# A windowed attention and two MLPs: first values in three loads of whole rows held twice, keys of the second group earlier, table load between loads

## The chip, the cores and the metric

The kernel runs on one core of a Trainium2 chip. A core has five engines with instruction streams of their own: TensorE (PE; its weight loads are listed as PEld), VectorE (DVE), ScalarE (ACT), GpSimd (POOL) and SyncE (SP), which here only issues loads and stores. The metric is the time of one execution on the device in microseconds, and the number compared is the median of the timed runs. One further execution was recorded by the hardware profiler.

## The reference

```python
scores = scale * np.matmul(q, k.transpose(0, 1, 3, 2))      # B,H,S,D = 4, 8, 576, 64
mask = (rel >= 0) & (rel < 128)                             # rel = query - key position
scores = np.where(mask, scores + bias[None], -1000000000.0) # bias = -slope[h] * |rel|
...
attn = attn / (np.sum(attn, axis=-1, keepdims=True) + 1e-09)
attn_out = np.matmul(attn, v)
x = attn_out.transpose(0, 2, 1, 3).reshape(2304, 512)
h = x @ moe_w_in;  x = np.maximum(0.01 * h, h) @ moe_w_out          # 512 -> 2048 -> 512
h = x @ moe2_w_in; y = (h * (1 / (1 + np.exp(-1.702 * h)))) @ moe2_w_out
```

Each query sees the 128 keys up to its own position. The weights of the two MLPs are given as 64-bit words.

## The kernel before, in words

**Attention.** The batches are taken in order; the 8 heads of a batch form two groups of four. The work of a group is cut into four parts of the 576 queries, so there are 32 steps (`steps`). The first eight steps take group 0 and group 1 of batch 0 in turns: steps 0, 2, 4, 6 are group 0, steps 1, 3, 5, 7 group 1. Step 0 and step 1 need the first 256 keys and queries of their group, steps 2 and 3 the rest.

A step is a pipeline over three turns of the loop at L533: in turn s, TensorE computes the scores of step s (`att_scores`, L253), the products with the values of step s-3 (`att_av`, L337) and the transposes of the softmax weights of step s-2 (`att_trans`, L302). VectorE adds the bias and takes the row maximum (`att_ttr`, L271), ScalarE takes the exponential (`att_exp`, L283), VectorE and GpSimd divide by the sum. The two transposed tiles of a step are copied from PSUM to the tile `pt` (`att_evac`): the first always by ScalarE (L310), the second by ScalarE in turns below 9 and by VectorE from turn 9 on (L312).

**Weights.** The raw blocks of the MLP weights (`raw`, 512 KB each, L115) are converted by nine operations spread over ScalarE, VectorE and GpSimd (`conv_w`, L136 to L148). In the attention's turns a turn starts a conversion where its number is in `convs`, and one group of MLP products of the first two chunks goes behind the attention's work of the turn. After the attention the MLP products fill TensorE (`steady`).

**Order of the work.** From L532 on the instructions stand on each engine in the order in which the code is written. What stands ahead of it (first loads, constants, warm-up products) is ordered by the framework. Each engine takes its instructions strictly in order, the queues of SyncE and ScalarE for loads as well. The framework gives the loads of both queues, in turn, eight completion counters; a load on a counter waits until the load that had this counter before has landed.

**The first loads.** `load_first` (L210) issues, on SyncE and ScalarE, queries and keys of group 0 (first part), of group 1 (first part), the rest of group 0, a raw block, the values of group 0, the rest of group 1, a raw block and the values of group 1. `q` comes in pieces of 64 numbers, 64 partitions to a load (L179). `k` comes with 128 partitions to a load (L185). The values of a group come in eight loads (L206): for each pair of heads, each head and each half of the 128 rows of a block, the rows of 64 numbers go to the 64 partitions at which the product with the weights wants them. A pair's two heads want the same keys at different halves of the partitions, so that the four products of a block can run on different quarters of TensorE's array. `values[b, g]` is the tile, and L339 picks `vv[r, a, kb]` from it.

The tile `ys` is the output of the MLPs; as long as it holds none, its columns serve as buffers: `late` holds queries, keys and values of the first group of batch 1, `kbuf` the keys, others are scratch of the conversions. The pool tag `v` has two buffers.

```python
    vv = (late[:, 2].rearrange("p a (n d) -> p a n d", d=64) if n == 2 else
          sb([128, 2, NKB, 64], F32, "v", 2))
```

Of the kernel before, what the change touches and what calls it, by code (L numbers as in the profile page):

```python
# [7 lines left out]
F32 = mybir.dt.float32  # L8
# [3 lines left out]
AF = mybir.ActivationFunctionType  # L12
ALU = mybir.AluOpType

B, H, S, D = 4, 8, 576, 64
# [5 lines left out]
CB = 2  # L21
# [3 lines left out]
NKB = S // 64  # L25
# [6 lines left out]
def attention_mlp_kernel(  # L32
        ctx: ExitStack, tc: tile.TileContext, qin, kin, v, w1i, w1o, w2i, w2o, out):
    nc = tc.nc
# [5 lines left out]
    def sb(shape, dt, tag, bufs):  # L40
        return pool.tile(shape, dt, tag=tag, name=tag, bufs=bufs)

    def ps(tag):
        return psum.tile([128, 512], F32, tag=tag, name=tag, bufs=2)
# [9 lines left out]
    def tick():  # L54
        step[0] += 1
        for fn in later.pop(step[0], []):
            fn()
# [12 lines left out]
    ys = const.tile([128, NT * 4], F32, name="y")  # L70
# [41 lines left out]
    def load_w(n, p):  # L112
        layer, f = divmod(n, NF)
        raw = sb([128, 1024], U32, "raw", 2)
        nc.sync.dma_start(out=raw, in_=wsrc[layer][p][f].bitcast(U32))  # L115
        wraw[n, p] = raw

    def alloc_w(n):
        wt[n] = wt[n - 2 * CB] if n >= 2 * CB else sb(
            [128, 4, 512], F32R, "wA" if n < CB else "wB", CB)  # L120
# [43 lines left out]
    qkv, values = {}, {}  # L164


    late = ys[:, 2560:2560 + 6 * S].rearrange("p (n a s) -> p n a s", n=3, a=2)

    def new_qk(n):
        qkv[divmod(n, 2)] = ((late[:, 0], late[:, 1]) if n == 2 else  # L170
                             (sb([128, 2, S], F32, "q", 2), kbuf[:, n % 2]))


    def load_q(e, n, a, lo, hi):
        b, g = divmod(n, 2)
        for h in range(2):
            d = slice(64 * h, 64 * h + 64)
            src = qin[b, 2 * g + a, d].rearrange("p (m h q) -> p m h q", h=2, q=64)
            e.dma_start(  # L179
                out=qkv[b, g][0][d, a, 64 * lo:64 * hi].rearrange("p (m q) -> p m q", q=64),  # L180
                in_=src[:, lo:hi, h])

    def load_k(n, lo, hi):
        b, g = divmod(n, 2)
        nc.sync.dma_start(  # L185
            out=qkv[b, g][1][:, :, 64 * lo:64 * hi],
            in_=kin[b, 2 * g:2 * g + 2, :, 64 * lo:64 * hi].rearrange("a p s -> p a s"))

    def load_qk(n):
        new_qk(n)  # L190
        for a in range(2):
            load_q(nc.sync, n, a, 0, NKB)
        load_k(n, 0, NKB)

    def load_v(n):
        b, g = divmod(n, 2)
        vv = (late[:, 2].rearrange("p a (n d) -> p a n d", d=64) if n == 2 else
              sb([128, 2, NKB, 64], F32, "v", 2))
        values[b, g] = vv

        for a in range(2):
            for h in range(2):
                for r in range(2):
                    src = v[b, 2 * g + a, 64 * r:64 * r + 64, 0:NQB - r, 64 * h:64 * h + 64]
                    k0 = 64 * (h ^ a)
                    nc.sync.dma_start(out=vv[k0:k0 + 64, a, r::2], in_=src)  # L206

    def load_first():  # L210
        for n in range(2):
            new_qk(n)
        load_q(nc.sync, 0, 0, 0, 4)
        load_q(nc.scalar, 0, 1, 0, 4)
        load_k(0, 0, 4)
        load_q(nc.scalar, 1, 0, 0, 4)
        load_q(nc.sync, 1, 1, 0, 4)
        load_k(1, 0, 4)
        for a in range(2):
            load_q(nc.scalar, 0, a, 4, NKB)  # L220
        load_k(0, 4, NKB)
        load_w(*wload.pop())
        load_v(0)
        for a in range(2):
            load_q(nc.sync, 1, a, 4, NKB)
        load_k(1, 4, NKB)
        load_w(*wload.pop())
        load_v(1)

    sp, sm, pp, pt, ot = {}, {}, {}, {}, {}  # L230
# [76 lines left out]
    def att_evac(s, n, e):  # L307
        t = sb([128, 384], F32, "pt", 3)
        if e is nc.scalar:
            nc.scalar.activation(t, pp.pop((s, n))[:, 0:384], AF.Copy)  # L310
        else:
            nc.vector.tensor_copy(t, pp.pop((s, n))[:, 0:384])  # L312
        pt[s, n] = t
# [4 lines left out]
    def att_av(s):  # L318
        b, g, i = steps[s]
        vv = values[b, g]  # L320
        ot[s] = [ps("O") for _ in range(2)]
        if i:
            todo = [(2 * i - 2 + c, 128 * c - (64 if c > 0 else 0), 128 * c + (64 if c < 3 else 0),
                     0 if c > 0 else 64, x == 0, x == 3) for x, c in enumerate((1, 2, 0, 3))]
        else:
            todo = [(m - w + 1 + c, 128 * (c0 + c), 0, 64 * x, c == 0, c == w - 1)
                    for x, (m, (_, w, c0)) in enumerate(zip((0, 1, 8), ENDS)) for c in range(w)]
        for kb, c0, c1, o0, start, stop in todo:
            for a in range(2):
                for h in range(2):  # L330
                    r = slice(64 * (h ^ a), 64 * (h ^ a) + 64)
                    if i:
                        rhs = pt[s, a][r, c0:c1]
                    else:
                        n, c = divmod(c0, 384)
                        rhs = pt[s, n][r, c + 64 * a:c + 64 * a + 64]
                    nc.tensor.matmul(  # L337
                        out=ot[s][a][64 * h:64 * h + 64, o0:o0 + rhs.shape[-1]],
                        lhsT=vv[r, a, kb], rhs=rhs, start=start, stop=stop,  # L339
                        skip_group_check=True,  # L340
                    )

# [174 lines left out]
            tick()  # L517


    wz = sb([128, 384], F32, "pt", 3)  # L520
    nc.gpsimd.memset(wz, 0.0)
    wp = ps("mm")
    for _ in range(6):
        nc.tensor.matmul(
            out=wp[:, 0:256], lhsT=wz[:, 0:128], rhs=wz[:, 128:384], start=True, stop=True)
    load_first()
    emit_consts()
    for n in range(2 * CB):
        alloc_w(n)
    convs = (0, 2, 4, 5, 7, 8, 10, 11)  # L530
    nconv, credit = 0, 0.0
    with tc.manual_schedule():  # L532
        for s in range(NS + 3):  # L533
            tick()
            todo, half = [], 0
            if s < NS:
                b, g, i = steps[s]
                nxt = 2 * b + g + 1 if b else 2 * B
                if nxt < 2 * B and i == 1:
                    load_qk(nxt)  # L540
                att_scores(s)
                if s == 4:
                    load_qk(2)
                todo = items(s)
                half = len(todo) // 2
            if s >= 3:
                att_av(s - 3)
            if s < NS and nxt < 2 * B and i == 3:
                load_v(nxt)
            if s == 5:  # L550
                load_v(2)
            tr = 2 <= s < NS + 2
            if tr:
                for n in range(2):
                    att_trans(s - 2, n)
            for x, p in todo[:half]:
                att_ttr(s, x, p)
            if 1 <= s <= NS:
                att_rcp(s - 1)
                for x, p in items(s - 1):  # L560
                    att_norm(s - 1, x, p)
            for x, p in todo[:half]:
                att_exp(s, x, p)
            tick()
            if s >= 3:
                att_hi(s - 3)
            if tr:
                att_evac(s - 2, 0, nc.scalar)
            for x, p in todo[half:]:
                att_ttr(s, x, p)  # L570
            if tr:
                att_evac(s - 2, 1, nc.scalar if s < 9 else nc.vector)
            tick()
            for x, p in todo[half:]:
                att_exp(s, x, p)
            if s >= 3:
                att_lo(s - 3)
            tick()
            if s in convs:
                conv_w(*wconv[nconv])  # L580
                nconv += 1
                if nconv < 4 * CB - 1:
                    load_w(*wload.pop())
            seen = S * ((s - 2) // 8) if s != 8 and s != 9 else TT
            credit += 1
            while credit >= 1:
                j, fn, x = groups[-1]
                layer, c, t = rounds[j]
                need = [(layer * NF + c * CB + f, int(fn is mm2)) for f in range(CB)]
                if not ready.issuperset(need) or fn is mm1 and (t + 1) * TT > seen:  # L590
                    credit = 0
                    break
                credit -= 1
                run_group()
                tick()
        window[0] = False
        steady(wconv[4 * CB:])
# [47 lines left out]
```

## Time and profile before

| | |
|---|---|
| median of three timed runs | 925.8 us (924.32 to 926.96) |
| profiled execution | 927.0 us, of which the span is 925.2 us |
| TensorE busy | 899.4 us (97% of the span) |
| TensorE weight loads busy | 841.6 us (91%) |
| VectorE busy | 564.0 us (61%) |
| ScalarE busy | 386.7 us (42%) |
| GpSimd busy | 392.3 us (42%) |
| mean granted clock of TensorE | 0.987 |

The shares are means over stages that differ. In the first tenth of the span (attention) VectorE and the loads are close to full and TensorE has gaps; in the rest TensorE has hardly any. [...] The span runs from the first to the last instruction; 1.8 us of the profiled execution lie around it.

### The profile page before, as it was taken

To read this page: it belongs to the slowest core of one execution; us is meant where nothing else is said; L and a number is where in the kernel's file an instruction comes from. 1 tells how busy PE (TensorE), PEld (TensorE's weight loads), DVE (VectorE), ACT (ScalarE), POOL (GpSimd) and SP (SyncE) were. 2 spreads that over 40 slices of the span, in tenths; PEclk is the share of its full clock that TensorE was granted. 3 is DMA by queue.
4 is the path that set the end of the run, shared out by engine and by line. 5 is a ranking of instruction groups with operands and counts; after the bars stand their busy time and mean duration, and the time that the engine had idled before them with its cause. 6 is when DMAs were issued, how large, how long until landed. Compare 5 with 4: busy or idle time off the path is not lost.

```text
span 925.2 us, 16379 instructions
## 1 busy us (share of the span) xinstructions
PE 899.4 (97%) x6252; PEld 841.6 (91%) x6252; DVE 564.0 (61%) x1220; ACT 386.7 (42%) x970; POOL 392.3 (42%) x448
## 2 busy tenths in 40 slices
PE   5789999999999999999999999999999999999998
PEld 4668989999999999999999998989898989898986
DVE  4998773159575655647384844667574848576333
ACT  3878885353333332323245545233332333333221
POOL 3777554234333333424268733424242424333221
PEclk7899999999999999999999999999999999999999
DMA  7764440012111110202020111102020201110034
GB/s 186 165 169 103 105 125 2 1 46 79 59 47 46 46 46 23 69 2 89 1 69 23 47 46 46 46 23 70 11 81 1 69 24 54 38 46 1 1 91 113
DMA packets 53421, 53.47 MB, mean 58 GB/s; under 512 B 40288, under 2 KB 41312, under 8 KB 53344
## 3 DMA queue, kind: packets, MB, share of 16 engines
q1 hardware_dynamic: 50912, 51.85, 20.2%
q8 instruction: 49, 0.80, 0.4%
q10 hardware_dynamic: 2432, 0.59, 0.3%
q14 instruction: 28, 0.23, 0.1%
HBM read 47.71 MB, written 4.72 MB: 57 GB/s over the span
## 4 chain that ended last, share of the span: by engine, by line
PE 93%; DVE 2%; DMA 2%; ACT 1%; SPq 1%; issue 0%; POOL 0%; DVEq 0%; POOLq 0%
PE pt L373 21%; PE S L373 20%; PE mm L419 15%; PE mm L410 12%; PE O L410 10%; PE O L419 7%; PE O L337 2%; PE pt L302 2%; PE S L253 2%; PE mm L373 2%; DMA y<-k 1%; DMA q<-q 1%; ACT st L283 0%; SPq L179 0%; DVE st L271 0%
## 5 line engine op out<-in xcount | busy, mean ns | idle before, releaser
L123 POOL TENSOR_TENSOR g<-u,g 128x384 fp32r<-128x384 f32 x192 | 202.7, 1056 | 436.1 <-ACT g L394 300.1
L394 ACT ACTIVATE g<-u 128x384 fp32r<-128x384 f32 x192 | 100.7, 525 | 47.3 <-DVE u L388 44.2
L430 DVE TENSOR_TENSOR y<-y,mm 128x384 f32<-128x384 f32 x88 | 48.5, 551 | 108.9 <-PE mm L410 80.0
L373 PE MATMUL pt<-x,wB 128*128 128x384 f32 x552 | 104.3, 337 | 0.0
L373 PE MATMUL pt<-x,wA 128*128 128x384 f32 x540 | 102.1, 337 | 0.0
L373 PE MATMUL S<-x,wA 128*128 128x384 f32 x540 | 101.9, 336 | 0.0
L373 PE MATMUL S<-x,wB 128*128 128x384 f32 x540 | 101.9, 336 | 0.0
L373 PEld LDWEIGHTS pt<-x,wB 128*128 128x128 f32 x552 | 97.9, 188 | 2.0
L147 POOL TENSOR_TENSOR ca<-ca,cb 128x512 f32<-128x512 f32 x59 | 82.0, 1391 | 39.4 <-DVE cb L145 37.3
L373 PEld LDWEIGHTS S<-x,wB 128*128 128x128 f32 x540 | 95.6, 188 | 2.2
L373 PEld LDWEIGHTS S<-x,wA 128*128 128x128 f32 x540 | 95.5, 188 | 2.1
L373 PEld LDWEIGHTS pt<-x,wA 128*128 128x128 f32 x540 | 95.8, 188 | 1.8
L384 ACT ACTIVATE u<-S 128x384 f32<-128x384 f32 x48 | 23.6, 492 | 132.0 <-PE S L373 132.0
L419 PE MATMUL mm<-wA,g 128*128 128x512 f32 x288 | 74.8, 395 | 0.0
L419 PE MATMUL mm<-wB,g 128*128 128x512 f32 x288 | 74.7, 395 | 0.0
L388 DVE SCALAR_TENSOR_TENSOR u<-u,pt 128x384 f32<-128x384 f32 x48 | 26.6, 554 | 70.7 <-ACT u L384 70.7
L435 DVE SCALAR_TENSOR_TENSOR y<-mm,y 128x512 f32<-128x512 f32 x84 | 57.8, 688 | 11.7 <-PE mm L419 11.7
L382 ACT ACTIVATE u<-S 128x384 f32<-128x384 f32 x42 | 20.7, 492 | 105.7 <-PE S L373 105.7
L388 DVE SCALAR_TENSOR_TENSOR u<-u,S 128x384 f32<-128x384 f32 x48 | 26.6, 555 | 62.1 <-ACT u L384 62.1
L410 PE MATMUL mm<-g,wA 128*128 128x384 f32 x312 | 63.9, 340 | 0.0
L410 PE MATMUL mm<-g,wB 128*128 128x384 f32 x312 | 63.6, 339 | 0.0
L419 PEld LDWEIGHTS mm<-wB,g 128*128 128x128 f32 x288 | 53.4, 188 | 9.2
(102 smaller groups left out, 1579.7 us busy)
## 6 DMA issues: line engine op xcount, KB each, us to landing
raw<-w1i SPq DMA_DIRECT2D x16, 512.0 KB, 3.6
raw<-w1o SPq DMA_DIRECT2D x16, 512.0 KB, 3.5
raw<-w2i SPq DMA_DIRECT2D x16, 512.0 KB, 3.5
raw<-w2o SPq DMA_DIRECT2D x16, 512.0 KB, 3.5
out<-y SPq DMA_DIRECT2D x36, 128.0 KB, 2.3
y<-k SPq DMA_DIRECT2D x6, 576.0 KB, 6.2
q<-q SPq DMA_DIRECT2D x20, 144.0 KB, 3.4
v<-v SPq DMA_DIRECT2D x28, 80.0 KB, 3.5
```

The lines of the kernel that those rows point to most:

```text
L123: e.tensor_tensor(out=out, in0=in0, in1=in1, op=ALU.subtract)
L147: lambda: nc.gpsimd.tensor_tensor(out=af, in0=af, in1=bf, op=ALU.add),
L253: nc.tensor.matmul(out=sp[s][bank][64 * u:64 * u + 64, col:col + 64 * w], lhsT=qq[d, a, 64 * m:64 * m + 64], rhs=kk[d, a, k1 - 64 * w:k1], ...
L373: nc.tensor.matmul(out=h, lhsT=w[:, a, k * 128:(k + 1) * 128], rhs=xs[:, b2, k, t0:t0 + TT], start=(m == 0), stop=(m == len(ops) - 1),)
L382: nc.scalar.activation(u, h, AF.Prelu, alpha=0.01)
L384: nc.scalar.activation(u, h, AF.Tanh, scale=0.851)
L388: nc.vector.scalar_tensor_tensor(out=u, in0=u, scalar=1.0, in1=h, op0=ALU.add, op1=ALU.mult)
L394: nc.scalar.activation(g[:, 0], u, AF.Copy)
L410: nc.tensor.matmul(out=yp, lhsT=wt[n0 + f][:, 2 + a, e * 128:(e + 1) * 128], rhs=gt[r, f][:, b2, :], start=(m == 0), stop=(m == len(ops) - 1),
L419: nc.tensor.matmul(out=y, lhsT=gt[r, f][:, b2, e * 128:(e + 1) * 128], rhs=wt[n0 + f][:, 2 + a, :], start=(m == 0), stop=(m == len(ops) - 1),)
L430: nc.vector.tensor_tensor(out=acc, in0=acc, in1=y, op=ALU.add)
L435: nc.vector.scalar_tensor_tensor(out=acc, in0=y, scalar=0.5, in1=acc, op0=ALU.mult, op1=ALU.add)
```

## The change

The first values (batch 0, group 0) are no longer loaded in eight loads of 64-number rows. `load_v_first` loads whole rows, all five blocks of a pair of heads with both heads side by side, 640 numbers to a row, into two areas of `ys`: one copy with the rows as they are (one load, 128 partitions), and one with the two halves of the partitions exchanged (two loads of 64 partitions). Where a product wants a value on the other half of the partitions, it reads the second copy: `find` gives the place. The rest of the values keeps its eight loads, reached through a small function. The values of batch 1's first group no longer lie in `ys` but in the pool `v`.

In `load_first` the first keys of group 1 are issued ahead of the queries of that group, the rest of its keys ahead of the rest of its queries; two loads of the rest of group 0's queries move from ScalarE's queue to SyncE's. ScalarE runs an exponential of one column between its second and third load, which brings the load of its function table to this place. The warm-up products of TensorE are five instead of six. All of this start is now inside the part whose order is as written. In turns 9 to 12 ScalarE instead of VectorE copies the second transposed tile.

```diff
@@ -164,7 +164,11 @@
-    late = ys[:, 2560:2560 + 6 * S].rearrange("p (n a s) -> p n a s", n=3, a=2)
+    late = ys[:, 2560:2560 + 4 * S].rearrange("p (n a s) -> p n a s", n=2, a=2)
+    vfirst = [ys[:, x:x + 10 * 128].rearrange("p (a n) -> p a n", a=2) for x in (0, 2560 + 4 * S)]
@@ -194,9 +198,8 @@
-        vv = (late[:, 2].rearrange("p a (n d) -> p a n d", d=64) if n == 2 else
-              sb([128, 2, NKB, 64], F32, "v", 2))
-        values[b, g] = vv
+        vv = sb([128, 2, NKB, 64], F32, "v", 2)
+        values[b, g] = lambda r, a, kb: vv[64 * r:64 * r + 64, a, kb]
@@ -205,25 +208,40 @@
-    def load_first():
+    def load_v_first():
+        src = v[0, 0:2].rearrange("a p n d -> p a (n d)")
+        nc.sync.dma_start(out=vfirst[0], in_=src)
+        for r in range(2):
+            nc.sync.dma_start(
+                out=vfirst[1][64 * r:64 * r + 64], in_=src[64 - 64 * r:128 - 64 * r])
+
+        def find(r, a, kb):
+            c = 128 * (kb // 2) + 64 * (r ^ a)
+            return vfirst[(kb ^ r) & 1][64 * r:64 * r + 64, a, c:c + 64]
+
+        values[0, 0] = find
+
+    def load_first(wz):
         for n in range(2):
             new_qk(n)
         load_q(nc.sync, 0, 0, 0, 4)
         load_q(nc.scalar, 0, 1, 0, 4)
         load_k(0, 0, 4)
+
+        nc.scalar.activation(wz[:, 0:1], wz[:, 1:2], AF.Exp)
+        load_k(1, 0, 4)
         load_q(nc.scalar, 1, 0, 0, 4)
         load_q(nc.sync, 1, 1, 0, 4)
-        load_k(1, 0, 4)
-        for a in range(2):
-            load_q(nc.scalar, 0, a, 4, NKB)
         load_k(0, 4, NKB)
+        load_q(nc.sync, 0, 0, 4, NKB)
+        load_q(nc.scalar, 0, 1, 4, NKB)
         load_w(*wload.pop())
-        load_v(0)
+        load_v_first()
+        load_k(1, 4, NKB)
         for a in range(2):
             load_q(nc.sync, 1, a, 4, NKB)
-        load_k(1, 4, NKB)
         load_w(*wload.pop())
         load_v(1)
@@ -336,7 +354,7 @@
-                        lhsT=vv[r, a, kb], rhs=rhs, start=start, stop=stop,
+                        lhsT=vv(h ^ a, a, kb), rhs=rhs, start=start, stop=stop,
@@ -517,19 +535,21 @@
-    for _ in range(6):
+        we = sb([128, 4, 6], F32, "sm", 5).rearrange("p a b -> p (a b)")
+        nc.gpsimd.memset(we, 0.0)
+        for _ in range(5):
...
-    load_first()
+        load_first(we)
@@ -569,7 +589,7 @@
-                att_evac(s - 2, 1, nc.scalar if s < 9 else nc.vector)
+                att_evac(s - 2, 1, nc.scalar if s < 13 else nc.vector)
```

The queue of SyncE at the start of the program, before (`y<-k` are keys, which lie in columns of `ys`; `raw<-w1i` is a block of raw weights; a row with x2 stands for two loads of one shape; the last load of values stands for six more of both shapes, left out):

```order
L179 DMA q<-q 64x4x64 x2
L185 DMA y<-k 128x2x256
L179 DMA q<-q 64x4x64 x2
L185 DMA y<-k 128x2x256
L185 DMA y<-k 128x2x320
L115 DMA raw<-w1i 128x1024
L206 DMA v<-v 64x5x64
L206 DMA v<-v 64x4x64
...
L179 DMA q<-q 64x5x64 x4
L185 DMA y<-k 128x2x320
L115 DMA raw<-w1i 128x1024
```

The same queue now, in the changed program's line numbers:

```order
L183 DMA q<-q 64x4x64 x2
L189 DMA y<-k 128x2x256 x2
L183 DMA q<-q 64x4x64 x2
L189 DMA y<-k 128x2x320
L183 DMA q<-q 64x5x64 x2
L115 DMA raw<-w1i 128x1024
L213 DMA y<-v 128x2x640
L215 DMA y<-v 64x2x640 x2
L189 DMA y<-k 128x2x320
L183 DMA q<-q 64x5x64 x4
L115 DMA raw<-w1i 128x1024
```

Eight loads of values became three larger ones, the last keys of group 1 moved ahead of four loads of queries, and two loads of queries of group 0 came over from ScalarE's queue.

ScalarE in turn 10, before (L353 takes the attention's output, L310 is the copy of a transposed tile, L148 and L136 belong to conversions):

```order
L283 ACTIVATE st_68,sm<-st_68,sm 128x3x64 x2
L353 ACTIVATE x<-O 128x128 x2
L310 ACTIVATE pt<-pt 128x384
L283 ACTIVATE st_68,sm<-st_68,sm 128x3x64 x2
L148 ACTIVATE wA<-y 128x512
L136 ACTIVATE ca<-raw 128x512
```

And now:

```order
L301 ACTIVATE st_68,sm<-st_68,sm 128x3x64 x2
L371 ACTIVATE x<-O 128x128 x2
L328 ACTIVATE pt<-pt 128x384 x2
L301 ACTIVATE st_68,sm<-st_68,sm 128x3x64 x2
L148 ACTIVATE wA<-y 128x512
L136 ACTIVATE ca<-raw 128x512
```

A second copy stands ahead of the second half of the exponentials and of the two conversions.

VectorE at the end of turn 11, before (L271 is bias and maximum of the step, L312 the copy, L141 to L145 a conversion, L123 the low part of the attention's output):

```order
L271 ISA y,sm<-S,biasp 128x3x64
L271 ISA sm 128x1
L312 COPY pt<-pt 128x384
L141 SCALAR_TENSOR_TENSOR ca<-raw,ca 128x512
L123 TENSOR_TENSOR x<-O,x 128x128 x2
L144 TENSOR_SCALAR cb<-ca 128x512
L145 SCALAR_TENSOR_TENSOR cb<-raw,cb 128x512
```

And now:

```order
L289 ISA y,sm<-S,biasp 128x3x64
L289 ISA sm 128x1
L141 SCALAR_TENSOR_TENSOR ca<-raw,ca 128x512
L123 TENSOR_TENSOR x<-O,x 128x128 x2
L144 TENSOR_SCALAR cb<-ca 128x512
L145 SCALAR_TENSOR_TENSOR cb<-raw,cb 128x512
```

The copy is gone from VectorE here, as in turns 9, 10 and 12; the rest keeps its order.

## Rows read from the trace of the kernel before

**Rows 1.** Stages: stretch, its length, each engine's busy us (instructions), granted clock, DMA share, GB/s.

```profile
core 0: us, PE busy (x) PEld busy (x) DVE busy (x) ACT busy (x) POOL busy (x), PEclk, DMA share, GB/s
...
43.50:74.30 30.80, 24.36 (x358) 20.36 (x351) 28.85 (x89) 23.71 (x83) 25.81 (x37) 1.00 0.71 173
74.30:77.70 3.40, 3.40 (x40) 3.28 (x41) 3.12 (x14) 2.10 (x10) 3.40 (x3) 0.50 0.12 24
77.70:100.00 22.30, 22.30 (x461) 19.92 (x460) 17.85 (x96) 19.03 (x82) 13.21 (x32) 1.00 0.31 78
...
200.00:924.00 724.00, 720.58 (x3830) 680.83 (x3828) 438.76 (x702) 253.87 (x495) 282.87 (x250) 1.00 0.15 46
```

**Rows 2.** Instructions of TensorE in time: start us, us, engine, line, tiles, [idle, releaser].

```profile
9.49 1.66 PE L253 MATMUL mm<-y,q 64*64 64x192 f32 x16 [2.02 <-DMA y<-k]
...
21.23 1.67 PE L253 MATMUL mm<-y,q 64*64 64x192 f32 x16 [5.75 <-DMA y<-k]
```

**Rows 3.** The same view, SyncE's queue: start and time of issuing.

```profile
7.83 6.83 SPq L206 DMA_DIRECT2D v<-v  x8
...
17.36 0.61 SPq L185 DMA_DIRECT2D y<-k  x1
```

**Rows 4.** The chain that ended last, 0 to 30 us: start us, us, what.

```profile
6.47 6.26 DMA q<-q
12.75 0.60 SPq L206
...
17.36 3.74 DMA y<-k
```

**Rows 5.** Instructions of ScalarE in time, 0 to 30 us.

```profile
7.78 1.28 ACT L283 ACT_TABLE_LOAD   x1 [7.78 <-DMA q<-q]
...
12.45 0.67 ACT L136 ACTIVATE ca<-raw 128x512 f32<-128x512 f32 x1 [1.50 <-DMA raw<-w1i]
...
23.79 0.68 ACT L136 ACTIVATE ca<-raw 128x512 f32<-128x512 f32 x1 [5.05 <-DMA raw<-w1i]
```

**Rows 6.** Stretches of the first 22 us, for what the loads moved.

```profile
0.00:6.00 6.00, 4.74 (x11) 3.86 (x12) 3.57 (x13) 0.00 (x0) 3.56 (x15) 1.00 0.50 124
2.00:12.00 10.00, 7.61 (x52) 5.47 (x50) 5.26 (x26) 3.15 (x9) 2.86 (x9) 0.87 0.93 235
12.00:13.00 1.00, 0.22 (x2) 0.23 (x4) 0.02 (x1) 0.55 (x1) 0.77 (x2) 0.50 1.15 183
13.00:20.00 7.00, 2.48 (x14) 1.49 (x12) 4.55 (x19) 4.60 (x19) 4.17 (x8) 0.50 0.55 122
20.00:22.00 2.00, 0.77 (x10) 0.80 (x14) 0.00 (x0) 0.00 (x0) 0.00 (x0) 0.50 1.05 345
```

**Rows 7.** The chain that ended last, 55 to 80 us: the copies.

```profile
59.92 0.38 ACT pt L310
...
66.76 0.47 DVE pt L312
...
72.77 0.47 DVE pt L312
```

**Rows 8.** Instructions of VectorE in time, 12 to 67 us.

```profile
14.21 0.42 DVE L139 TENSOR_SCALAR ca<-ca 128x512 uint32<-128x512 uint32 x1
...
17.71 0.09 DVE L271 DVE_READ_ACCUMULATOR2_ANT sm<- 128x1 f32 x1
...
62.37 1.24 DVE L137 TENSOR_SCALAR ca<-ca 128x512 f32<-128x512 f32 x1 [1.24 <-ACT ca L136]
...
64.91 1.08 DVE L139 TENSOR_SCALAR ca<-ca 128x512 uint32<-128x512 uint32 x1
```

**Rows 9.** Instructions of TensorE in time, 70 to 110 us: products with the values.

```profile
74.26 1.74 PE L337 MATMUL O<-pt,y 64*64 64x128 f32 x32 [0.57 <-DVE x L123]
79.30 0.88 PE L337 MATMUL O<-pt,y 64*64 64x64 f32 x48
...
86.00 0.85 PE L337 MATMUL O<-pt,v 64*64 64x128 f32 x32
89.34 0.85 PE L337 MATMUL O<-pt,v 64*64 64x128 f32 x32
```

More of the change, by code (lines that the diff above doesn't have):

```diff
@@ L517, in steady @@
             tick()
-    wz = sb([128, 384], F32, "pt", 3)
-    nc.gpsimd.memset(wz, 0.0)
-    wp = ps("mm")
-    for _ in range(6):
-        nc.tensor.matmul(
-            out=wp[:, 0:256], lhsT=wz[:, 0:128], rhs=wz[:, 128:384], start=True, stop=True)
-    load_first()
-    emit_consts()
-    for n in range(2 * CB):
-        alloc_w(n)
     convs = (0, 2, 4, 5, 7, 8, 10, 11)
@@ L532, in attention_mlp_kernel @@
     with tc.manual_schedule():
+        wz = sb([128, 384], F32, "pt", 3)
+        nc.gpsimd.memset(wz, 0.0)
+        we = sb([128, 4, 6], F32, "sm", 5).rearrange("p a b -> p (a b)")
+        nc.gpsimd.memset(we, 0.0)
+        wp = ps("mm")
+        for _ in range(5):
+            nc.tensor.matmul(
+                out=wp[:, 0:256], lhsT=wz[:, 0:128], rhs=wz[:, 128:384], start=True, stop=True)
+        load_first(we)
+        emit_consts()
+        for n in range(2 * CB):
+            alloc_w(n)
         for s in range(NS + 3):
```

## Prediction

> **What bounds the kernel now.** I read the stages first, then TensorE's waits, then the chain that ended last, and only then the queues.
>
> The stages [rows 1] show that nearly the whole span is TensorE at work: from 200 to 924 us it is busy 720.6 of 724 us, and from 77.7 us on it hardly stops. Nothing in the change touches what it computes there, so whatever is won before 77.7 us moves the end by the same amount, and nothing else does. Before that, from 43.5 to 74.3 us, VectorE is the full engine, 28.85 of 30.80 us.
>
> TensorE's waits at the start [rows 2] have one that stands out: the scores of the fourth step (group 1, second half of the keys) begin at 21.23 us after 5.75 us of idling, released by the load of `k`. The sync queue [rows 3] shows why it is late. Eight loads of `v` begin at 7.83 us and take 6.83 us to issue, four of `q` follow, and the wanted `k` load is issued only at 17.36 us. The chain [rows 4] confirms it: issued at 17.36, it lands 3.74 us later, at 21.10. It also shows something that the queue alone hides. A load of `q` takes 6.26 us to land (6.47 to 12.73), and the sync queue's next load starts at 12.75 us: the loads take turns on eight counters, and one waits until the load eight places ahead of it has landed.
>
> ScalarE [rows 5] has the second gate of the same place. Its conversion of the second raw weight block starts at 23.79 us after 5.05 us of idling for that load, and VectorE's conversions follow behind it. Both, the scores at 21.23 and the raw block at 23.79, must come earlier, or the later one holds the rest.
>
> **The change, part by part.**
>
> *Loads.* Before the values, the new order issues the same bytes as the old one: eight `q` loads of 64 KB, four of 80 KB, two `k` of 256 KB, one of 320 KB and one raw block of 512 KB, together 2176 KB (from the shapes in the order rows, 4 bytes an element) or 2228 kB. From 2 to 12 us the engines moved 235 GB/s [rows 6], so these are through at 2 + 2228/235 = 11.5 us, and the values can begin to move.
>
> The values grow from 576 KB in eight loads to 1280 KB (1311 kB) in three: each row of 640 numbers, twice. The first copy writes 128 partitions in rows of 2560 bytes. The nearest row is 20 to 22 us, where `k` and raw rows of 1280 and 4096 bytes into 128 partitions moved at 345 GB/s: 655/345 = 1.9 us. The second copy comes in two halves of 64 partitions each, and no row shows a long load of that form. Its upper bound is 12 to 13 us, when loads of `q` and `v` into 64 partitions in pieces of 256 bytes moved 183 GB/s: 3.6 us; its lower bound is 345 GB/s again, 1.9 us. I take 3.2 us, close to the 183 row because that one has the same half of the partitions, and a little under it because the rows are ten times as long. [...]
>
> Then the keys of group 1, 328 kB at 345 GB/s, 0.95 us, and its four `q` loads, 328 kB at 183 GB/s, 1.8 us. Now it is `q` that comes last. From the last byte to the landing I add 0.85 us, worked out from before: 2176 + 576 + 320 + 320 KB, 3473 kB, precede and include that `k`; 2350 kB are through by 12 us, 183 by 13 and 854 by 20, the rest at 345 GB/s by 20.25, and it landed at 21.10. So the fourth step may start at 11.5 + 1.9 + 3.2 + 0.95 + 1.8 + 0.85 = 20.2 us instead of 21.1: **0.9 us earlier** (2.2 with the lower bound, 0.5 with the upper one). Five issues of 0.6 us on the sync queue fall away as well, but they are not the term. Now the data engines, not the queue, are the bound, since the last `q` can be issued by 14 us: its turn among the eight open loads comes when the first raw block lands, near 12.4 us as before [rows 5].
>
> The second raw block came 2.7 us after the `k` (21.10 to 23.79). It now stands right behind the last `q`, so I keep the 2.7 us, and it gains the same 0.9. The eight loads of group 1's values stand behind it as before.
>
> *Table load.* It took 1.28 us at 7.78, just ahead of the first exponentials [rows 5]. It now runs between issues on ScalarE. I count nothing: the exponentials of the second step stand behind the conversion at 12.45 us, which waits 1.50 us for the raw block anyway. If that cover went, at most the 1.28 us would be won. The `q` loads that it delays on ScalarE's queue by the same 1.28 us are needed for the second step, which begins at 9.49 [rows 2], far ahead of the gate at 20.2.
>
> *One warm-up product fewer, another memset.* Both lie ahead of the first scores, and the second step's scores still wait 2.02 us for their load, until 9.49 us [rows 2]. Nothing.
>
> *Evacuations.* In turns 9 to 12 one copy of 128x384 goes from VectorE to ScalarE. Two of the four lie on the chain, at 66.76 and 72.77 us, 0.47 us each [rows 7], with VectorE's other work back to back around them: **0.94 us won**. ScalarE, busy 23.71 of the 30.80 us of this stretch [rows 1], has room for the copies while VectorE works. In turn 9 neither side is on the chain. In turn 10 ScalarE is: its one copy takes 0.38 us of the chain at 59.92, the conversion behind it starts that much later with a second one, and VectorE has idled 1.24 us for that conversion at 62.37 [rows 8]. **0.38 us lost.**
>
> *Values of batch 1 in the common pool.* The loads of a later group now wait on the sync queue until a later step of the group before has released the buffer, and the raw loads and the next `q` and `k` stand behind them. But these loads are issued at the end of the very step that releases it. I count nothing; if a raw load came late by it, ScalarE's conversion would wait the same tenths.
>
> *Sum.* -0.9 - 0.94 + 0.38 = -1.5 us. Against the profiled execution, 927.0 us (925.2 of span and 1.8 around it), this is 925.5. That execution is as slow as the slowest of the three timed runs, whose median is 925.8, so on the median I forecast **924.3 us**. Its own range is 923.2 to 925.4: 0.4 either way for the second copy, and 0.66 for how VectorE's and GpSimd's work falls together. The same kind of operation took 0.42 us at 14.21 and 1.08 us at 64.91 [rows 8], so a shifted start can give or take such 0.66 us.
>
> **The rivals.**
>
> [...]
>
> *The loads run at the good rate throughout.* Both copies at 345 GB/s: the start gains 2.2 instead of 0.9, and the time is 923.0. For: the long rows. Against: the half partitions.
>
> [...]
>
> *The start is held elsewhere.* VectorE's work on the third step ends at 17.8 us [rows 8]; if that slipped by 3 us, the earlier load would be hidden, and only the evacuations' 0.6 is left: 925.2. Against: they hang on the first raw block, which keeps its place in bytes.
>
> *Slower: the doubled values choke the queue.* The place is the same, the 1311 kB ahead of keys, `q` and raw block. If they move only as fast as the first 6 us did, 124 GB/s [rows 6], they take 10.6 us instead of 5.1, and the time is 924.3 + 5.5 = 929.8. It is slower than before from 6.6 us on (199 GB/s), and measurably so from 9.4 us (140 GB/s). Against: that row holds the queue's start, with few loads issued.
>
> **How the numbers follow.** About 0.3% of this time, 2.8 us, can be told from no change: faster means under 923.0, slower over 928.6. Forecast 0.38, high clock 0.20, good rate 0.18, half rate 0.12, held elsewhere 0.05, slower 0.07. Under 923.0 lie most of the high clock (0.17), half of the good rate (0.09), and a rest of the forecast where VectorE's shift and the runs' own scatter of 1.3 us to each side help (0.08): 0.34. Slower is 0.07, the rest 0.59. The range takes in the high clock below with a little scatter, 921.8, and above the forecast's end with its scatter and the start held elsewhere, 926.3; the choked queue stays out.
>
> **What would show it.** The fourth step's scores start between 18.8 and 20.6 us, released by `q`. The second raw block's conversion starts near 22.9. No exponential waits for the table load any more. The copies of turns 9 to 12 stand in ScalarE's rows and TensorE's dense stretch begins 1.5 us sooner. It is wrong if the scores still start after 21 us, if the dense stretch does not move with them, or if TensorE's stretch after 77.7 us changes its length.

## The result, and the profile after

The changed kernel takes 917.97 us (median of four runs, 917.70 to 918.21), the kernel before beside it 926.38 (924.32 to 927.04): ratio 0.9913, 95% interval 0.9896 to 0.993. That is 8.4 us faster, 6.3 us under the 924.3 of the forecast and below its range (921.8 to 926.3). The profiled execution took 918.11 us, its span 916.3, at a mean granted clock of 0.985.

TensorE's waits at the start, after (columns as in [rows 2]):

```profile
7.71 1.30 PE L271 MATMUL mm<-y,q 64*64 64x192 f32 x12 [0.29 <-DMA y<-k]
...
19.54 1.95 PE L271 MATMUL mm<-y,q 64*64 64x192 f32 x16 [5.81 <-DMA q<-q]
```

The fourth step's scores begin at 19.54 us in place of 21.23 and are released by `q`. SyncE's queue, as in [rows 3]:

```profile
9.00 0.61 SPq L115 DMA_DIRECT2D raw<-w1i  x1
9.65 0.43 SPq L213 DMA_DIRECT2D y<-v  x1
10.12 1.37 SPq L215 DMA_DIRECT2D y<-v  x2
11.53 0.61 SPq L189 DMA_DIRECT2D y<-k  x1
12.19 2.63 SPq L183 DMA_DIRECT2D q<-q  x4
15.32 0.35 SPq L115 DMA_DIRECT2D raw<-w1i  x1
```

The wanted keys are issued at 11.53 us (17.36 before). The chain of the first 22 us, as in [rows 4], now runs through the values to the second raw block, and on into ScalarE's conversion; before, it ran through the keys into the scores:

```profile
3.13 4.54 DMA y<-k
...
9.65 5.66 DMA y<-v
...
15.32 6.63 DMA raw<-w1i
```

The second raw block is issued when the first copy of the values has landed (15.31). ScalarE, as in [rows 5]:

```profile
2.20 1.28 ACT L233 ACT_TABLE_LOAD   x1 [2.20 <-issue]
2.26 1.67 ACTq L183 DMA_DIRECT2D q<-q  x2
...
13.31 0.66 ACT L136 ACTIVATE ca<-raw 128x512 f32<-128x512 f32 x1 [3.60 <-DMA raw<-w1i]
...
21.98 0.67 ACT L136 ACTIVATE ca<-raw 128x512 f32<-128x512 f32 x1 [2.56 <-DMA raw<-w1i]
...
64.71 0.86 ACT L328 ACTIVATE pt<-pt 128x384 f32<-128x384 f32 x2
```

The first raw block's conversion came 0.86 us later than before, the second's 1.81 us earlier. Stretches after, to set beside [rows 1, 6]:

```profile
2.00:12.00 10.00, 7.54 (x58) 4.68 (x56) 5.11 (x26) 3.35 (x10) 4.49 (x13) 1.00 0.88 203
13.30:15.30 2.00, 0.43 (x3) 0.03 (x1) 1.30 (x6) 1.99 (x8) 0.00 (x0) 0.50 1.06 338
15.30:18.10 2.80, 0.00 (x0) 0.00 (x0) 2.70 (x11) 1.71 (x8) 0.58 (x1) 0.50 1.06 246
...
66.60:70.00 3.40, 3.40 (x40) 3.28 (x37) 3.33 (x10) 3.37 (x13) 2.35 (x3) 0.50 0.74 212
```

The first copy of the values moved at 338 GB/s, the halves at 246. TensorE had its stretch at a granted clock of 0.50 again, 66.6 to 70.0 us. (The last two figures of such a row are the DMA share and GB/s, the one before them the granted clock.)

The surprise stands in the part that nobody meant to change. TensorE in the MLP, before:

```profile
121.78 1.29 PE L410 MATMUL mm<-g,wA 128*128 128x384 f32 x6
...
525.62 1.56 PE L419 MATMUL mm<-wA,g 128*128 128x512 f32 x6
...
703.42 1.56 PE L419 MATMUL O<-wB,g 128*128 128x512 f32 x6
704.82 2.26 PE L373 MATMUL S<-x,wB 128*128 128x384 f32 x12
706.92 1.55 PE L419 MATMUL mm<-wB,g 128*128 128x512 f32 x6
...
919.02 1.56 PE L419 MATMUL mm<-wB,g 128*128 128x512 f32 x6
```

and after:

```profile
118.88 1.32 PE L428 MATMUL mm<-g,wA 128*128 128x384 f32 x6
...
519.81 1.54 PE L437 MATMUL mm<-wA,g 128*128 128x512 f32 x6
...
704.23 1.52 PE L437 MATMUL O<-wB,g 128*128 128x512 f32 x6
705.59 2.28 PE L391 MATMUL S<-x,wA 128*128 128x384 f32 x12
707.71 1.52 PE L437 MATMUL mm<-wB,g 128*128 128x512 f32 x6
...
909.35 1.52 PE L437 MATMUL mm<-wB,g 128*128 128x512 f32 x6
```

The first and last rows are the same products of the program in both, and TensorE hardly idles between them (busy 797.15 of 797.24 us before, 790.39 of 790.47 after). The lead of the changed kernel is 2.90 us at the first (121.78 - 118.88), 5.81 at the first product of the second layer and 9.67 at the last. So 2.9 us of the gain in these two profiles come from the start, 2.91 from the first layer of the MLP and 3.86 from the second; 0.8 us are given back behind the last products, where the output leaves (925.2 - 919.02 before, 916.3 - 909.35 after). The pieces in the middle show how: from one start to the next, six products of 512 columns take 1.40 us before (704.82 - 703.42) and 1.36 after, at the same clock (1.00 from 200 us to the end of the products, both). Twelve products of 384 columns take 2.10 before and 2.12 after. The instructions are the same; each (a *pass* below) takes a few nanoseconds more or less.

What differs is where their operands lie. Before, the five small tiles `sm` (96 B a partition each) are set up in the first step, behind the weights. The change takes a sixth use of `sm`, the tile `we` of the early table load, ahead of `q`; so the pool sets the five up there, and `q`, `raw`, `v`, `wA` and `wB` all move up by 480 B. `x`, `y`, `u` and `g` stay. Every pass has a stationary operand (`lhsT` in the kernel), for which the trace has a weight load (one group of the page before has 552 loads of 128x128, 188 ns each, beside its 552 products of 128x384), and a streamed one (`rhs`). The passes that read `x` have weights stationary and stream `x`; those that read `g` have weights stationary and stream `g` in the first MLP, and the other way round in the second.

### The profile page after: what moved, and what is told of

It is laid out like the page before. It is cut to its first block, busy times and chain, and to the rows that moved or that the text cites. A ratio compares the mean times of both kernels' runs of the same rounds, so it can differ in the third digit from the quotient of the medians.

```text
span 916.3 us, 16365 instructions
## 1 busy us (share of the span) xinstructions
PE 893.8 (98%) x6250; PEld 840.6 (92%) x6250; DVE 559.6 (61%) x1216; ACT 387.4 (42%) x975; POOL 392.9 (43%) x449
## 4 chain that ended last, share of the span: by engine, by line
PE 93%; DVE 2%; DMA 2%; ACT 1%; issue 1%; SPq 0%; POOL 0%; DVEq 0%; POOLq 0%
PE pt L391 21%; PE S L391 21%; PE mm L437 14%; PE mm L428 12%; PE O L428 10%; PE O L437 7%; PE O L355 2%; PE pt L320 2%; PE mm L391 2%; PE S L271 2%; DMA raw<-w1i 1%; DMA y<-v 1%; DMA y<-k 0%; DVE st L289 0%; ACT st L301 0%
## 5 line engine op out<-in xcount | busy, mean ns | idle before, releaser
L123 POOL TENSOR_TENSOR g<-u,g 128x384 fp32r<-128x384 f32 x192 | 202.5, 1055 | 430.6 <-ACT g L412 289.1
L453 DVE SCALAR_TENSOR_TENSOR y<-mm,y 128x512 f32<-128x512 f32 x84 | 57.7, 687 | 10.2 <-PE mm L437 10.2
```

Of the source, the lines that this page charges most:

```text
L123: e.tensor_tensor(out=out, in0=in0, in1=in1, op=ALU.subtract)
L453: nc.vector.scalar_tensor_tensor(out=acc, in0=y, scalar=0.5, in1=acc, op0=ALU.mult, op1=ALU.add)
```

## Experiments

Each kernel's time is the median of its timed runs; ratios are to the kernel before on the same chip. A "layer" below is one of the two MLPs, measured like the rows above: first layer from the product at 121.78 us in the kernel before to the second layer's first, second layer from there to the last six products. The profile tells these lengths to a few hundredths of a microsecond.

**e1, e2: only the places.** e1 is the kernel after without the move, e2 the kernel before with nothing else:

```diff
-        we = sb([128, 4, 6], F32, "sm", 5).rearrange("p a b -> p (a b)")
+        we = ys[:, 1280:1304]
```

```diff
+    we = sb([128, 4, 6], F32, "sm", 5)
+    nc.gpsimd.memset(we, 0.0)
     load_first()
```

> The kernel after, with the small tile of the early table load put into an unused piece of y, so that no place in SBUF moves: q, raw, v and the weights wA and wB lie 480 B lower, where they lay in the kernel before. Theory A (the places of the operands make the MLP faster): the start's gain stays and the MLP's 6.6 us go back, about 924.6 us, and the 512-column products are at 395 ns again (389 in the kernel after). Theory B (the loads or the copies of the change, or the chip, make it faster): 918.0 us and 389 ns.

> The kernel before, with one unused tile of the tag sm set up ahead of q, and nothing else: every tile lies where it lies in the kernel after, all instructions and transfers but one memset on GpSimd are those of before. Theory A (places): 926.4 - 6.6 = 919.8 us and 389 ns for a 512-column product. Theory B: 926.4 us and 395 ns.

e1: 924.90 us, 0.9988 (0.9979 to 0.9997). e2: 919.85 us, 0.993 (0.9913 to 0.9946). Theory A holds in both directions, B falls. TensorE in e1:

```profile
523.60 1.56 PE L437 MATMUL mm<-wA,g 128*128 128x512 f32 x6
...
917.00 1.56 PE L437 MATMUL mm<-wB,g 128*128 128x512 f32 x6
```

The second layer is 393.40 us long again, as before, with all of the change's loads and copies in.

**e3 to e6: which tiles.** Unused bytes, or the five `sm`, moved to one place each:

```diff
# e3: the kernel before, behind load_first() and ahead of the weights
+    sb([128, 4, 6], F32, "sm", 5)
# e4 (8 numbers, 32 B), e5 (24 numbers, 96 B): the kernel before; e6 (8): the kernel after; ahead of the first g
+            if not gt:
+                sb([128, 8], F32, "pad", 1)
             g = sb([128, 2, TT], F32R, "g", 5)
```

> The kernel before with the five sm tiles set up between v and wA: only the weights wA and wB lie 480 B higher, the landing buffers q, raw and v stay at their old places. Theory A1 (the place of the weights that TensorE reads): 919.8 us, 389 ns. Theory A2 (the landing buffers, that is the DMA writes and the conversion's reads): 926.4 us, 395 ns. Mixed: between.

> The kernel before with 32 unused bytes ahead of the five g tiles: the weights stay at a multiple of 64 B, g moves from 32 B past such a multiple onto one. Theory A1 (absolute place of the weights): no change, 926.4 us and 395 ns. Theory A3 (what counts is that weights and g stand alike to a 64-B line, which they do in the kernel after and here): 919.8 us and 389 ns. If g's own place counts for itself, the 384-column products that stream g change (336 ns) while the 512-column ones stay.

> The kernel before with 96 unused bytes ahead of the five g tiles: weights at a multiple of 128 B, g 64 B past one (it was 96 B past one, and at 0 in the run with 32 bytes). Theory A64 (weights and g must stand alike in a 64-B line): fast as with g at 0, about 919.3 us. Theory A128 (alike in a 128-B line): slow as before, 926.0 us and 395 ns.

> The kernel after with 32 unused bytes ahead of the g tiles: weights 32 B past a multiple of 64 B, g on one. Theory A (alike): they differ again, so the MLP's gain goes back though every line of the change is in: 918.0 + 6.6 = 924.6 us. Theory A' (it is enough that either of the two has moved from where it lay before): 918.0 us.

e3: 919.75 us, 0.9932 (0.9917 to 0.9946): the weights alone do it. e4: 919.20, 0.9928 (0.9913 to 0.9943): moving `g` alone, with every weight at its old place, does it too. So it is the place of one operand to the other. e5: 924.04, 0.9982 (0.9973 to 0.9991), between its two theories: second layer as slow as before (393.40 us), first 1.8 us shorter. e6: 922.34, 0.997 (0.9958 to 0.9982), 2.3 us under the forecast of 924.6: the second layer lost more than its gain (394.56 us), the first kept its own (400.29). "Alike or not" was too simple.

**e7 to e10: with x.**

```diff
# e7: x up by 32 B, weights and g up by 64
+    const.tile([128, 8], F32, name="padx")
     xs = const.tile([128, 2, 4, NT], F32R, name="x")
# e7 (8), e9 (16), e10 (24 numbers), ahead of the weights
+        sb([128, 8], F32, "pad", 1)
         for n in range(2 * CB):
             alloc_w(n)
# e8: we in y as in e1, and 8 numbers ahead of the first u
```

> The kernel after with x, weights and g all 32 B past a multiple of 64 B (x 32 B up, weights and g kept alike). Theory A also for the first products, which take weights and x: their 2304 passes at about 173.4 ns from start to start in place of 175.2, 4 us less, about 914 us. If x's place does not matter, or only that of weights and g: 918.0 us.

> The kernel after with x, weights, u and g all on a multiple of 64 B (the small tile put into y, 32 unused bytes ahead of u). Theory A: all alike, as in the run before it, about 914 us. By the run that moved g alone in the kernel before (919.2 against 926.0 us): 924.9 - 6.8 = 918.1 us, if u's place does not matter.

> The kernel after with 64 unused bytes ahead of the weights: weights and g keep their distance, but stand 32 B past a multiple of 128 in place of 96, x stays at 0. Theory: only the distances of x, weights and g count (three kernels with all three alike, at 0 or at 32, had the same times of each pass). If the best distance of x to the weights is 96 as in the kernel after: slower, up to 918.6. If a distance that was not tried is better in the first products (2304 passes at 173.4 ns in place of 175.2): about 914 us.

> The same with 96 unused bytes: weights and g 64 B past a multiple of 128, x at 0. Between 914 us (a better distance) and 918.6 us; if only the 64-B line counts, as the all-alike kernels: 918.1 us, and passes as in them (229, 233, 234, 225, 229 ns in the 512-column products).

e7: 918.10 us, 0.9922 (0.9906 to 0.9939). e8: 918.04, 0.9921 (0.9907 to 0.9936). e9: 917.96, 0.9916 (0.9901 to 0.9931). e10: 919.21, 0.9932 (0.9917 to 0.9947). None reached 914 us, but e4, e7 and e8, with the three tiles alike (within 256 B, e7's stand 32 B further on than those of e4 and e8), have layers of the same length, and e9 has the shortest second layer of all and a first layer as long as before.

**e13, e14: a place for each layer.** Longer weight and `g` tiles, read 32 B further on in the second layer, and 8 numbers ahead of the first `u`; e13 has `we` in `y` as in e1, and e14 is the same in the kernel before.

```diff
...
-            [128, 4, 512], F32R, "wA" if n < CB else "wB", CB)
+            [128, 4 * 512 + 32], F32R, "wA" if n < CB else "wB", CB)
+        o = 8 if n >= NF else 0
+        wt[n] = wbase[n][:, o:o + 2048].rearrange("p (a c) -> p a c", a=4)
...
```

> The kernel after with a place for each layer, as the passes of the earlier runs point to: x, weights, u and g on multiples of 128 B in the first layer (every pass was at 173.3 to 173.7 ns there), weights and g 32 B past one in the second (173.8 and 226.7 ns there). Each weight and g tile is 128 B longer for it; the work is the same. Theory (distances among x, weights and g set the time of each pass): second layer from 390.7 to 387.6 us, first layer 0.5 us less, 918.0 - 3.6 = 914.4 us. Rival (the place of the tiles in SBUF as a whole, or what lies beside them): 918 us.

> The kernel before with the places of the run before it and nothing of the change in loads or copies. Theory: the places alone give 6.6 + 3.6 us and the start of the kernel before stays, 925.8 - 10.2 + 0.2 = about 916 us. The difference to the run before it is what the loads and copies of the change are worth: 1.5 us by the forecast. If most of the start's gain was also places: the same time as the run before it.

e13: 923.58 us, 0.9972 (0.9963 to 0.9982); e14: 925.56, 0.9997 (0.9988 to 1.0006). A miss by 9 us: tiles longer by 128 B put the four weight tiles, and the five `g`, at places that differ by 128 B from one to the next. If the distance is what counts, it counts over more than 128 B; e17 tries that by itself. The difference of the two, 2.0 us, is what the loads and copies are worth at equal places.

**e16 to e18: how far the distance counts.** e17 and e18 are e8 with 128 and 256 unused bytes ahead of the weights. e16 is e13 with every weight tile 512 B longer (the last 32 B), the second layer's `g` in the tiles of `q` and `v` (four in place of five), and the two scratch tiles `st` joined in one:

```diff
...
+            wbase[n] = pool.tile([128, 2048 + (128 if n < 3 else 8)], F32R,
+                                 tag="w%d" % n, name="wA" if n < CB else "wB", bufs=1)
...
+                    gring.extend(sb([128, 2 * S], F32R, tag, 2) for tag in "qqvv")
+                g = gring[gnum[0] % 4][:, 8:8 + 2 * TT].rearrange("p (a c) -> p a c", a=2)
```

> The kernel of e8 with 128 unused bytes ahead of the weights: weights, u and g 128 B further on, x where it was. If distances count within 128 B: passes as in e8 (first products 174.7 ns on average in the second layer, 512-column products 229, 233, 234, 225, 229 ns). If within 256 B or 512 B: other passes, as in e13.

> The kernel of e8 with 256 unused bytes ahead of the weights. If distances count within 256 B: passes as in e8. If within 512 B: other passes.

> The kernel after with a place for each layer as in e13, but with every tile kept at the same place within 512 B: x, weights, u and g 128 B past a multiple of 512 in the first layer, weights and g 160 B past one in the second; the second layer's g tiles lie in the four tiles of q and v, idle by then (four in turn in place of five). Theory (distances of x, weights and g within a line of more than 128 B; e13 failed because its longer tiles stood at four different places): second layer 390.7 to 387.6 us, first 0.5 us less, 914.4 us. Rival (the distances are not what counts): 918 to 924 us.

e17 took 922.85 us and e18 917.96 (one run each). Groups of TensorE from 540 to 900 us (behind the busy time the mean recorded length of one in ns; recorded lengths overlap, so they are longer than the 227 to 233 and 173 to 177 ns from one start to the next), e8:

```profile
L439 PE MATMUL mm<-wA,g 128*128 128x512 f32 x258 | 66.7, 394 | 0.0
...
L391 PE MATMUL pt<-x,wB 128*128 128x384 f32 x276 | 51.6, 334 | 0.0
```

e18:

```profile
L439 PE MATMUL mm<-wA,g 128*128 128x512 f32 x258 | 66.7, 394 | 0.0
...
L391 PE MATMUL pt<-x,wB 128*128 128x384 f32 x276 | 51.6, 334 | 0.0
```

e17:

```profile
L439 PE MATMUL mm<-wA,g 128*128 128x512 f32 x264 | 67.6, 392 | 0.0
...
L391 PE MATMUL pt<-x,wB 128*128 128x384 f32 x276 | 52.1, 338 | 0.0
```

256 B further nothing has changed, at 128 B it has. e16 took **914.98 us, 0.9885 (0.9867 to 0.9903)**: faster than both kernels, where 914.4 was expected. Its two layers are 3.63 us shorter than those of the kernel after, for 3.6 forecast. TensorE in e16:

```profile
518.74 1.52 PE L449 MATMUL mm<-wA,q 128*128 128x512 f32 x6
...
701.68 1.52 PE L449 MATMUL O<-wB,q 128*128 128x512 f32 x6
703.04 2.25 PE L397 MATMUL S<-x,wA 128*128 128x384 f32 x12
705.12 1.52 PE L449 MATMUL mm<-wB,q 128*128 128x512 f32 x6
...
905.20 1.52 PE L449 MATMUL mm<-wB,v 128*128 128x512 f32 x6
```

Six products of 512 columns in 1.36 us and twelve of 384 in 2.08, the best of either kernel at once; the second layer is 386.46 us long (905.20 - 518.74). All layers, by the places within 256 B (in bytes):

| weights minus x | g minus weights | first layer, us | second layer, us | kernels |
|---|---|---|---|---|
| 0 | -32 | 403.84 to 403.86 | 393.40 | before, e1 |
| -32 | 0 | 400.92 to 400.94 | 389.53 to 389.54 | after, e2, e3, e11, e12, e15 |
| 0 | 0 | 400.30 to 400.38 | 390.48 | e4, e7, e8, e18 |
| 0 | +64 | 402.06 | 393.40 | e5 |
| -32 | +32 | 400.29 | 394.56 | e6 |
| +32 | 0 | 403.87 | 386.46 | e9 |
| +64 | 0 | 401.05 | 389.56 | e10 |
| 128 | 0 | 404.00 | 389.54 | e17 |
| 0, then +32 | 0 | 400.38 | 386.46 | e16 |
| 0 and 128, then +32 and 160 | several | 403.95 to 403.96 | 391.86 to 391.87 | e13, e14 |

**e11, e12, e15: the parts of the start.**

```diff
# e11: the first values in eight loads again, in the same piece of y
-        load_v_first()
+        load_v(0)
# e12
-        nc.scalar.activation(wz[:, 0:1], wz[:, 1:2], AF.Exp)
# e15
-                att_evac(s - 2, 1, nc.scalar if s < 13 else nc.vector)
+                att_evac(s - 2, 1, nc.scalar if s < 9 else nc.vector)
```

> The kernel after with the first values loaded as before, in eight transfers of 256-B rows held once, into the same unused piece of y; the order of all other loads, the early table load and the copies as after. If the form of the values' transfers wins the start (the forecast's 0.9 us, or the 1.7 us that the profile shows): fourth step's scores at 20.4 to 21.2 us and 918.9 to 919.7 us. If the order of the other loads wins it: 19.5 us and 918.0 us.

> The kernel after without the early small exponential, so that the function table is loaded at the first real exponential; the small tile stays, so all places do. Forecast: the table load is worth nothing, 918.0 us, with the first exponential 1.2 us later (9.1 in place of 7.8 us) and the fourth step's scores still at 19.5 us. Rival: the 1.28 us are on the path of the first steps, 919.2 us.

> The kernel after with the second copy of each turn given to VectorE from the tenth turn on, as before (s < 9 in place of s < 13). Forecast: the copies on ScalarE are worth 0.56 us between 60 and 78 us, so about 918.5 us, and the lead over the kernel before grows by nothing in that stretch (in the kernel after from 2.4 to 2.9 us). Rival: TensorE had slack there, 918.0 us and the same lead.

e11: 919.26 us (918.12 to 921.25), 0.9935 (0.9919 to 0.995); inconclusive against the kernel after's 0.9913 (0.9896 to 0.993). Its profile has the fourth step's scores begin at 18.68 us, earlier than in the kernel after, and the last of them wait for `q` until 20.69:

```profile
18.68 1.68 PE L272 MATMUL mm<-y,q 64*64 64x192 f32 x12 [3.77 <-DMA q<-q]
20.69 0.58 PE L272 MATMUL mm<-y,q 64*64 64x192 f32 x2 [0.33 <-DMA q<-q]
...
21.06 0.53 PE L272 MATMUL mm<-y,q 64*64 64x192 f32 x2
```

They end at 21.59 us, those of the kernel after at 21.49 (19.54 + 1.95). So in this profile, of the shortest of its executions, the order of the other loads alone gives nearly all of the earlier scores; by the median, 1.3 us over that of the kernel after, the form of the values would be worth what was forecast. Which of the two it is stays open. In the same profile the product at 121.78 us before starts at 119.12, 0.24 later than after.

e12: 917.22 us (916.29 to 919.32), 0.9907 (0.989 to 0.9923): no loss is seen without the early table load. ScalarE and the fourth step's scores in e12:

```profile
5.88 1.28 ACT L300 ACT_TABLE_LOAD   x1 [5.88 <-DMA q<-q]
8.68 0.45 ACT L300 ACTIVATE st<-st,sm 128x192 f32<-128x192 f32 x1 [1.51 <-DVE sm L288]
...
21.61 1.66 PE L270 MATMUL mm<-y,q 64*64 64x192 f32 x14 [6.86 <-DMA q<-q]
```

The table load lies in a wait, and the first exponential waits another 1.51 us for VectorE. The scores, expected at 19.5 us, came at 21.61: the last four `q` loads took 5.08 us to issue (11.18 to 16.26) in place of 2.63. This profile is of the longest of the four executions, 919.32 us, and whether the others had it too is not known.

e15: 918.80 us (917.34 to 920.67), 0.9919 (0.9907 to 0.9932): the sign of the forecast's 0.56 us, within the scatter, so not settled. Its profile, of the longest of its five executions, leads the kernel before by 0.27 us at the product at 121.78, where 2.4 was expected.

## Why the prediction was wrong

**The step that failed** is the first: "Nothing in the change touches what it computes there, so whatever is won before 77.7 us moves the end by the same amount, and nothing else does." The first half is true, the second is not. The time of the same products hangs on where the weights lie to `x` and `g`, and a tile of 96 B for the table load moved the weights against both. That is 6.9 us by e1 against after, 6.2 by e2 against before and 6.77 by the lengths of both layers (403.84 + 393.40 - 400.94 - 389.53), over four times all that I had summed. I costed the early table load as an instruction and a memset, and never asked where its tile is put. The closing sentence, that a change in the length of TensorE's stretch after 77.7 us would prove it wrong, named the place. The time came out under the 923.0 to which I gave a chance of 0.34, but by none of the causes that I had counted towards it.

**The sum of the start came out about right, in part by luck.** With places equal, the change is worth 1.1 us (e1 against before), 1.9 (after against e2, across two sets of runs) and 2.0 (e13 against e14), for 1.5 forecast. (The 2.9 us above is one pair of profiles; the product at 84.08 us before starts 1.8 us earlier on average over the profiles of either start that are compared below.) e1, 924.9 us, is the kernel that I had predicted at 924.3. But the sum holds one term at half its size and one that no run shows:

- *Loads, 0.9 us: the size was off.* In the six profiles with the old start (before, e2 to e5, e14) the fourth step's scores begin at 20.95 to 22.57 us, mean 21.55. In the twelve with all of the change's loads (after, e1, e6 to e10, e13, e15 to e18) it is 19.10 to 20.55, mean 19.79. That is 1.8; at the end of these scores it is 1.4. My times along the way missed in both directions: 203 GB/s from 2 to 12 us, not 235, so the first raw block landed at 13.3 us and the values began there, not at 11.5; they took 4.8 us (13.3 to 18.1) for 5.1. I gained it at the end, for the scores began with the first of the last `q` loads and did not wait for all four. Whether the order of the loads gained it or the form of the values, on which my working turned, e11 leaves open.
- *Half rate of the halves (0.12 of the chances):* not seen. By all that moved in the two stretches the halves came at 246 GB/s against the first copy's 338, 0.73 of it; half would be 169.
- *Second raw block:* it came 2.4 us after the scores' start as before (2.6), at 21.98 for the 22.9 forecast. In the profile after, the chain runs through it and not through the scores.
- *Table load:* nothing, as forecast, so far as e12 shows. The load of `q` behind it on ScalarE's queue did not wait for it: it was issued at 2.26 us, while the table load ran from 2.20 to 3.48.
- *Copies, 0.56 us: not seen.* From the start of the fourth step's scores to the product at 84.08 us before, the six profiles of the old start take 61.9 us on average (61.3 to 62.9), the eleven with the change's loads and copies 62.0 (61.6 to 62.7). e15, with the loads and without the copies, takes 63.4 in its one profile, which is of the longest of its five executions. So the term is neither shown nor excluded.
- *High clock (0.20 of the chances): no gain from it is seen.* The step that ran in part at a granted clock of 0.50 took 5.04 us (74.26 to 79.30), a later one at 1.00 3.34 (86.00 to 89.34) [rows 1, 9]; the 1.7 us between them, my estimate of the gain, are also in the range's low end. No run shows such a gain. The clock differs between executions of nearly the same instructions. Two stretches (columns as in [rows 1]) of before and then of e5, which differ only in 96 unused bytes:

```profile
36.00:52.00 16.00, 12.55 (x216) 9.78 (x212) 15.32 (x48) 12.99 (x45) 14.27 (x20) 0.89 0.49 134
52.00:84.00 32.00, 27.12 (x412) 23.72 (x411) 28.41 (x106) 24.09 (x90) 25.79 (x38) 0.95 0.61 146
```

```profile
36.00:52.00 16.00, 11.06 (x219) 8.75 (x214) 15.33 (x48) 13.06 (x46) 14.27 (x20) 1.00 0.51 142
52.00:84.00 32.00, 27.17 (x418) 23.61 (x417) 29.18 (x112) 24.84 (x94) 26.60 (x41) 1.00 0.61 149
```

  The granted clock fell to 0.50 for 3.4 us in each stretch of the first and not at all in the second. The stretch from scores to product took 62.85 us and 61.83. But e3, with 6.8 us at 0.50 between 36 and 84 us, took 61.31, and the kernel after, with 10.2 us, 61.65; so the clock doesn't explain the scatter. Over whole executions the clock is higher with the change: its mean is 0.991 to 0.994 in every kernel with the change's loads and several executions, 0.986 to 0.989 in every one with the old ones. The time does not follow it: the executions of e1 with the lowest and the highest clock of its ten, 0.986 and 0.999, took 924.94 and 925.66 us.
- *Choked queue, start held elsewhere:* neither happened.

Open: why the places matter. In these runs the time goes with the distances of `x`, weights and `g` within 256 B (400.29 to 404.00 us for the first layer, 386.46 to 394.56 for the second), and moving `q`, `raw` and `v` (e2 against e3, layers alike within 0.02 us) or `u` (e4 against e8, within 0.08) changed nothing. `x` and `y` were never moved apart; I name `x` because TensorE reads it in these products. Whether it is TensorE's own two reads that meet was not tried.

## What to carry to other kernels

Where one engine is full for most of the span, compare the time of one of its instructions before and after, not only the idle time: a few ns in a pass were worth more here (6.2 to 6.9 us) than every wait that the change removed (1.1 to 2.0). Before costing an edit, look for what it allocates, and ahead of what; one tile set up earlier moved `q`, `raw`, `v` and the weights by 480 B here. When a matmul-bound kernel is tuned, try a few unused multiples of 32 B ahead of the streamed and the stationary tiles, keep the lengths of their buffers a multiple of 256 B (a shift of 256 B left both layers as they were in e18; with weight and `g` tiles longer by 128 B e13 took 923.58 us, with three weight tiles longer by 512 B e16 took 914.98), and choose by the pass times in a single profile.

## What was not expected of the hardware

The same 512-column pass took 1.40/6 = 233 ns or 1.36/6 = 227 ns, and a 384-column pass 2.08/12 = 173 to 2.12/12 = 177 ns, at the same granted clock (1.00), with the distance of operands within 256 B of a partition; the lengths of a layer repeat to within 0.1 us over kernels of the same distances. The best and the worst of the two layers seen differ by 400.29 + 386.46 against 404.00 + 394.56, 11.8 us or 1.5% of them.
